# Moving stores from ScalarE's queue to SyncE's in a fused attention and feed-forward kernel

## The chip, the cores and the metric

One NeuronCore of a Trainium2 chip runs the kernel. The metric is device time in microseconds for one execution; a kernel's figure is the median of several runs. Names: PE is TensorE, PEld its loading of weights, DVE is VectorE, ACT is ScalarE, POOL is GpSimd, SP is SyncE. ACT and SP can both issue DMA transfers; their queues are called ACTq and SPq in the trace. "L1283" is a line of that kernel's source, so the numbers differ between kernels.

## The reference

Attention with normalised queries and keys (8 batches, 12 heads, 448 tokens, 64 wide), and a gated feed-forward layer on its output (3584 tokens, 768 to 1536 to 768). The three weight matrices come in as 8-byte floats.

```python
q_n, k_n = rmsnorm(q, g_q), rmsnorm(k, g_k)
attn = softmax(q_n @ k_n.T / 8)                 # 8 x 12 x 448 x 448
x = (attn @ v).transpose(0, 2, 1, 3).reshape(3584, 768)
g = x @ w_gate
out = (g * sigmoid(g) * (x @ w_val)) @ w_out
```

## The kernel before

Each matrix product of the feed-forward layer is made as a 3 x 3 scheme of blocks with 15 products in place of 27. Each product needs a combination of weight blocks, a "side". So the weights are first converted: 24 conversions each load nine 128 x 128 blocks of 8-byte numbers, round them to 4 bytes (two passes on ACT, six on DVE), add and subtract blocks on POOL, and store 15 sides to DRAM. The feed-forward blocks load the sides from there in pieces. Four of the 15 sides are plain weight blocks.

A small planner in the kernel places every piece of work: a piece names its engine, its estimated time, its wished time and what it follows, and the planner fixes the order on each engine at build time. The engines then work strictly in that order.

The program falls into stretches: the early attention (12 pairs of heads, with the first six conversions), then four times an "up" block (480 products, gate and value) and a "down" block (240 products, mixed with the next attention), the last down block alone. The other 18 conversions run in the first up block.

The store of a conversion, in five issues because the plain blocks lie apart from the others; `by_bank` is true for the 18 conversions of the first up block:

```python
queue = nc.scalar if by_bank else nc.sync

def store():
    for i, j, k, m in ((3, 6, 6, 2), (2, 5, 12, 9)):
        queue.dma_start(pair(to, at[k], at[m]), pair(blocks, i, j))
    holes = [*sorted(at[x] for x in (6, 2, 12, 9)), 15]
    for i, j in zip(holes, holes[1:]):
        if j - i > 1:
            queue.dma_start(to[:, i + 1 : j], sides[:, i + 1 : j])

last = add(
    "ACT" if by_bank else "SP", 1.75 if by_bank else 3.0, when, store, after=[last], kb=960
)
```

The store of results, four issues of 56 KB for each transposed tile:

```python
def store():
    for q4 in range(P // C):
        to = out[ds(b * S, S), ds((2 * nn + s) * P + C * q4, C)]
        queue = nc.sync if n == NB - 1 and q4 % 2 else nc.scalar
        queue.dma_start(...)
add("ACT", 1.4 if n < NB - 1 else 0.7, when + 1.4, store, after=[turned], uses=[rows], kb=224)
```

ACT, which issues these, also computes: the exponentials of the attention, the silu of the up blocks, copies out of the matrix banks, and the first two passes of each conversion.

Of the kernel before, what the change touches and what calls it, by code (L numbers as in the profile page):

```python
# [477 lines left out]
def fast(  # L478
# [127 lines left out]
    FRESH = (2, 6, 8, 12, 9)  # L606
    up_sides = [dram.tile([P, 15, 2, NC2, P], F32, name=f"up_sides{g}") for g in range(NG)]
# [89 lines left out]
    def attention(m):  # L697
# [19 lines left out]
        def load(x, src):  # L717
            def emit():
                to = take("qk", (m, x), [P, NC, C])
                for g in range(P // C):  # L720
                    rows = src[b, 2 * c + g // 2][:, ts(g % 2, C)]
                    queue.dma_start(to[ts(g, C)], rows.rearrange("(c i) f -> i c f", i=C))


            both = m < 3 and src is k
            queue = nc.scalar if both else nc.sync
            return add(
                "ACT" if both else "SP", 1.4 if both else 2.4, ready - 28.0, emit, takes=[("qk", (m, x))], kb=224, early=25.0,
                after=[staged.get(PAIRS)],
            )  # L730
# [364 lines left out]
    def convert(key, src, order_of, to, when, place, by_bank):  # L1095
# [6 lines left out]
        dst, raw = places[place][:, 0:VALUES], places[place][:, VALUES:PLACE]  # L1102
# [4 lines left out]
        def load():  # L1107
            to = raw.bitcast(I64).rearrange("p (k n f) -> p k n f", k=3, n=3)
            for k in range(3):
                nc.sync.dma_start(to[:, k], src(k))  # L1110

        loaded = add(
            "SP", 1.8, when - 12.0, load, after=[staged.get(place), *wait], kb=1152, early=3.0
# [41 lines left out]
        alls = raw.rearrange("p (b f) -> p b f", f=P)  # L1155
        sides = alls[:, 0:15]
        b11, b12, b13, b21, b22, b23, b31, b32, b33 = (blocks[:, i] for i in range(9))
        at = {x: i for i, x in enumerate(order_of)}
# [8 lines left out]
        def pair(x, i, j):  # L1167
            return x[:, i : j + 1 : j - i]
# [4 lines left out]

        spare = raw[:, 15 * P : 16 * P]
        for us, op in (
            (0.79, plus(pair(sides, at[10], at[4]), pair(blocks, 1, 7), pair(blocks, 2, 8))),
            (0.79, plus(pair(sides, at[6], at[1]), twice(w[10]), pair(blocks, 0, 3))),
            (0.48, plus(w[14], w[6], b31)),
            (0.48, minus(w[13], b22, w[10])),
            (0.48, minus(w[8], w[4], b23)),  # L1180
            (0.48, plus(w[7], b21, b22)),
            (0.48, minus(w[7], w[8], w[7])),
            (0.79, minus(pair(sides, at[2], at[3]), twice(b13), pair(blocks, 3, 6))),
            (0.48, plus(w[5], w[2], b11)),
            (0.79, minus(pair(alls, at[11], 15), pair(blocks, 7, 8), pair(blocks, 2, 5))),
            (0.48, plus(w[0], spare, b31)),
        ):
            last = add("POOL", us, when, op, after=[last], port=True)


        queue = nc.scalar if by_bank else nc.sync

        def store():
            for i, j, k, m in ((3, 6, 6, 2), (2, 5, 12, 9)):
                queue.dma_start(pair(to, at[k], at[m]), pair(blocks, i, j))
            holes = [*sorted(at[x] for x in (6, 2, 12, 9)), 15]
            for i, j in zip(holes, holes[1:]):
                if j - i > 1:
                    queue.dma_start(to[:, i + 1 : j], sides[:, i + 1 : j])

        last = add(
            "ACT" if by_bank else "SP", 1.75 if by_bank else 3.0, when, store, after=[last], kb=960
# [4 lines left out]
    def up_weights(i, *how):  # L1207

        g, which, c = i // 4, i // 2 % 2, i % 2
        w = (moe_w_gate, moe_w_val)[which].rearrange("(c k p) (n f) -> p c k n f", p=P, k=3, n=3)  # L1210
        weights["up", i] = convert(
            ("up", i), lambda k: w[:, c, k, :, ts(g, P)], UP_ORDER, up_sides[g][:, :, which, c], *how
        )

    def down_weights(i, *how):

        g, s = divmod(i, 2)
        w = moe_w_out.rearrange("(k g p) (n s f) -> p k g n s f", g=NG, p=P, n=3, s=2)
        weights["down", i] = convert(
            ("down", i), lambda k: w[:, k, g, :, s], DOWN_ORDER, down_sides[:, :, s, g], *how  # L1220
        )
# [29 lines left out]

    def block(n):
# [12 lines left out]
        def up_product(g, step, x, which, load, key):  # L1265
# [4 lines left out]
            opens = which and g == 0 and step < 2  # L1270
            bank = (which, b)
# [6 lines left out]
            def emit():  # L1278
                if opens:
                    take(*value_banks[b], [P, TB])  # L1280
                w = tiles[key].rearrange("p (x w c f) -> p x w c f", x=5, w=2, c=NC2)
                for c in range(NC2):
                    nc.tensor.matmul(  # L1283
                        ps(), w[:, step % 5, which, c], xs[:, SLOT[x], c],
                        start=fresh and c == 0, stop=c == NC2 - 1, skip_group_check=True,
                    )
# [87 lines left out]
        def up_load(g, piece):  # L1374
            key = ("ws", (n, g, piece))
            load = add(
                "SP", 0.6, start + (30 * g + 10 * piece) * unit - 24.0,
                lambda: nc.sync.dma_start(
                    take(*key, [P, 10 * NC2 * P]),
                    up_sides[g][:, ts(piece, 5)].rearrange("p x w c f -> p (x w c f)"),  # L1380
                ),
                after=[*last_load, *(weights["up", 4 * g + i] for i in range(4))], takes=[key], kb=1280,
                early=8.0,
            )
            last_load[:] = [load]
            return key, load
# [52 lines left out]
        def down_product(step, x, s):  # L1439
# [5 lines left out]
            if piece not in loads:  # L1445
                loads[piece] = add(
                    "SP", 0.6, when - 24.0,
                    lambda: nc.sync.dma_start(
                        take(*key, [P, 10 * NC2 * P])[:, 0 : size * 2 * NG * P],
                        down_sides[:, ds(2 * piece, size)].rearrange("p x s g f -> p (x s g f)"),  # L1450
                    ),
# [6 lines left out]
            def emit():  # L1458
                w = tiles[key][:, 0 : size * 2 * NG * P]
                w = w.rearrange("p (x s g f) -> p x s g f", s=2, g=NG, f=P)  # L1460
                for g in range(NG):
                    nc.tensor.matmul(  # L1462
                        banks[s][:, 0:S], w[:, step % 2, s, g], where[x][:, g],
                        start=fresh and g == 0, stop=g == NG - 1, skip_group_check=True,
                    )
# [50 lines left out]
            def store():  # L1516
                for q4 in range(P // C):
                    to = out[ds(b * S, S), ds((2 * nn + s) * P + C * q4, C)]
                    queue = nc.sync if n == NB - 1 and q4 % 2 else nc.scalar
# [6 lines left out]
                "ACT", 1.4 if n < NB - 1 else 0.7, when + 1.4, store, after=[turned], uses=[rows],  # L1526
# [30 lines left out]
    for t, x in ((gq2, g_q), (gk2, g_k)):  # L1557
        col = x.rearrange("(d one) -> d one", one=1)
        nc.scalar.dma_start(t[0:64, :], col)
        nc.scalar.dma_start(t[64:128, :], col)  # L1560
# [95 lines left out]
```

## Time and profile before

| | us |
|---|---|
| median of 4 runs, in the rounds with the changed kernel | 1533.06 (1528.9 to 1538.2) |
| span of the profiled execution | 1529.4 |
| TensorE busy in it | 1439.6 (94%) |

The first view is the busy time by stretch, cut where TensorE's work changes kind: the stretch and its length, then busy us (and instructions) of PE, PEld, DVE, ACT and POOL, the mean granted clock of TensorE (1.00 is full speed), the DMA share (the mean busy share of the 16 DMA engines) and GB/s. Shown are the early attention, the first up block, the second down block and the third up block.

```profile
0.00:152.00 152.00, 110.42 (x1201) 49.39 (x1202) 99.59 (x175) 92.35 (x181) 57.50 (x92) 0.97 0.68 164
152.00:367.50 215.50, 190.66 (x490) 92.09 (x489) 158.16 (x239) 87.87 (x127) 115.02 (x207) 0.95 0.82 253
...
730.40:890.30 159.90, 156.57 (x988) 70.65 (x984) 112.10 (x161) 98.15 (x223) 62.90 (x38) 0.99 0.43 96
890.30:1088.00 197.70, 194.19 (x601) 95.97 (x601) 92.30 (x159) 70.88 (x135) 11.52 (x10) 0.98 0.35 101
```

The length less PE's busy time is idle time: 41.6, 24.8, 3.3 and 3.5 us here. A clock below 1.00 means that part of PE's busy time is slow work.

The second view is the timeline: start, duration, engine, line, operation, and in brackets how long the engine had been idle and what ended it.

```profile
878.55 8.54 ACTq L1520 DMA_DIRECT2D out_dram<-spare  x8
880.22 9.84 SPq L1378 DMA_DIRECT2D ws<-up_sides  x2
...
887.14 0.53 ACT L989 COPY xs<-at 128x448 f32<-128x448 f32 x1 [8.87 <-DMA out_dram<-spare]
...
894.83 1.86 PE L1283 MATMUL mm<-xs,ws 128*128 128x448 f32 x2 [3.48 <-DVE xs L1030]
```

Eight issues of results keep ACT's queue for 8.54 us. The issues themselves take 4.1 us of this. The longest wait between two of them, 3.2 us, ends at 886.77, which is 0.02 us after the first of SP's two loads of sides (1.28 MB, issued at 880.22) has landed; the second load is issued only at 889.74. So ACT's issue seems to wait for a transfer of another queue; why is not shown. The copy of an attention result, next in ACT's order, waits 8.87 us for them, and through VectorE's division and combinations TensorE waits 3.48 us.

### The profile page before, as it was taken

The page shows a single profiled execution, that of the slowest core. Times are in us where ns is not written, and L with a number is a line of the kernel's source. Part 1 is how long each engine was busy: PE and PEld are TensorE (multiplying, and loading weights), DVE is VectorE, ACT ScalarE, POOL GpSimd, SP SyncE. Part 2 cuts the span into 40 slices and gives each one's busy share as a digit, 9 for nine tenths or more (in the row PEclk, how much of TensorE's full clock was granted, in tenths as well). Part 3 has the DMA queues.
Part 4 walks back from the last instruction along what each step waited for, and adds up shares of the span by engine and source line. Part 5 has one row for each costly group of instructions (what it writes and reads, how often), then busy time and mean ns, then how long its engine had stood idle before and what let it go on. Part 6 is the DMA issues. An engine that isn't in the chain of part 4 may idle for free.

```text
span 1529.4 us, 19374 instructions
## 1 busy us (share of the span) xinstructions
PE 1439.6 (94%) x6672; PEld 683.1 (45%) x6672; DVE 912.1 (60%) x1405; ACT 679.7 (44%) x1366; POOL 397.0 (26%) x440
## 2 busy tenths in 40 slices
PE   3888989879999999999999989999999989999998
PEld 1334444434444445554444445554444435555554
DVE  3868877667886743455886643444786744323533
ACT  5765434335876422255776422135767532222100
POOL 1553755553543300002444300002344310000000
PEclk9999999989999999999999999999999999999999
DMA  7567888974454342343454342343344342222235
GB/s 152 132 152 223 274 290 270 292 206 133 105 105 106 65 143 75 112 113 88 101 120 98 60 127 69 109 113 109 79 111 109 78 110 89 85 101 72 83 95 104
DMA packets 408240, 193.28 MB, mean 126 GB/s; under 512 B 324164, under 2 KB 397892, under 8 KB 398404
## 3 DMA queue, kind: packets, MB, share of 16 engines
q1 hardware_dynamic: 288288, 163.92, 38.6%
q10 hardware_dynamic: 119844, 28.04, 8.5%
q8 instruction: 54, 0.88, 0.3%
q14 instruction: 54, 0.44, 0.1%
HBM read 157.29 MB, written 34.60 MB: 125 GB/s over the span
## 4 chain that ended last, share of the span: by engine, by line
PE 65%; DVE 5%; ACT 2%; issue 2%; DMA 1%; ACTq 1%; SPq 1%; POOL 0%; DVEq 0%; POOLq 0%
PE mm L1283 18%; PE at L1283 18%; PE mm L1462 18%; PE st L834 5%; PE at L910 4%; ACTq L1520 1%; PE st L934 1%; ACT spare L984 1%; ACT es L849 1%; DMA out_dram<-spare 1%; DVE spare L1510 1%; DVE sums L860 1%; DVE rd L969 1%; DMA ws<-down_sides 0%; DVE xs L996 0%
## 5 line engine op out<-in xcount | busy, mean ns | idle before, releaser
L1283 PE MATMUL mm<-xs,ws 128*128 128x448 f32 x960 | 409.4, 549 | 30.4 <-DVE gt L1250 17.2
L1283 PE MATMUL at<-xs,ws 128*128 128x448 f32 x960 | 404.7, 544 | 2.7 <-DVE v L1248 1.6
L1283 PEld LDWEIGHTS mm<-xs,ws 128*128 128x128 f32 x960 | 182.8, 192 | 218.4 <-issue 167.2
L1283 PEld LDWEIGHTS at<-xs,ws 128*128 128x128 f32 x960 | 183.9, 192 | 186.5 <-issue 177.3
L789 POOL TENSOR_TENSOR work<-work,rr 128x448 f32<-128x448 f32 x96 | 99.1, 1053 | 539.2 <-DVE rr L680 377.6
L834 PE MATMUL st<-work 64*64 64x448 f32 (+1 forms) x1536 | 154.6, 508 | 29.3 <-ACT work L808 20.4
L1462 PE MATMUL mm<-gt,ws 128*128 128x448 f32 x448 | 177.4, 548 | 0.0
L1246 DVE TENSOR_TENSOR gt<-gt,mm 128x448 f32<-128x448 f32 x64 | 39.7, 620 | 207.2 <-PE mm L1283 200.2
L1462 PE MATMUL mm<-hs,ws 128*128 128x448 f32 x384 | 151.0, 544 | 0.0
L849 ACT ACTIVATE es<-st 128x896 f32<-128x896 f32 x129 | 114.4, 914 | 80.0 <-PE at L910 31.0
L1357 ACT ACTIVATE st<-gt 128x448 f32<-128x448 f32 x96 | 52.5, 547 | 205.1 <-DVE gt L1250 96.2
L984 ACT COPY spare<-rd 32x224 f32<-32x224 f32 x288 | 108.1, 375 | 40.0 <-DVE rd L969 34.9
L854 POOL TENSOR_TENSOR sums<-es 128x896 f32<-128x896 f32 x36 | 75.2, 2089 | 180.4 <-PE st L934 82.0
L1462 PEld LDWEIGHTS mm<-gt,ws 128*128 128x128 f32 x448 | 84.2, 191 | 84.4 <-issue 82.6
L910 PE MATMUL at<-es,v 64*64 64x448 f32 x1032 | 112.6, 543 | 4.5 <-ACT es L849 2.6
L1244 ACT COPY gt<-mm 128x448 f32<-128x448 f32 x80 | 42.5, 531 | 156.8 <-PE mm L1283 153.0
L1462 PEld LDWEIGHTS mm<-hs,ws 128*128 128x128 f32 x384 | 71.3, 190 | 71.8 <-issue 70.1
L834 PEld LDWEIGHTS st<-work 64*64 64x64 f32 x1536 | 51.7, 134 | 104.8 <-issue 36.3
L1244 ACT COPY v<-at 128x448 f32<-128x448 f32 x96 | 51.0, 532 | 82.1 <-PE at L1283 65.3
L805 DVE STREAM_TRANSPOSE work<-work 128x448 f32<-128x448 f32 x96 | 59.7, 632 | 29.8 <-POOL work L789 21.1
L854 POOL TENSOR_TENSOR sums<-sums,es 128x896 f32<-128x896 f32 x36 | 75.7, 2103 | 2.8
L1360 DVE SCALAR_TENSOR_TENSOR gt<-st,v 128x448 f32<-128x448 f32 x96 | 59.7, 622 | 16.9 <-ACT st L1357 10.0
(137 smaller groups left out, 1541.9 us busy)
## 6 DMA issues: line engine op xcount, KB each, us to landing
ws<-up_sides SPq DMA_DIRECT2D x48, 1280.0 KB, 5.7
ws<-down_sides SPq DMA_DIRECT2D x28, 1024.0 KB, 5.0
work<-in_q_dram SPq DMA_DIRECT2D x192, 56.0 KB, 2.5
work<-in_k_dram SPq DMA_DIRECT2D x180, 56.0 KB, 2.4
out_dram<-spare ACTq DMA_DIRECT2D x168, 56.0 KB, 2.0
v<-in_v_dram SPq DMA_DIRECT2D x96, 96.0 KB, 2.5
es<-in_moe_w_out_dram SPq DMA_DIRECT2D x9, 384.0 KB, 6.6
v<-in_v_dram SPq DMA_DIRECT2D x96, 32.0 KB, 2.3
```

The source lines that it names most:

```text
L789: nc.gpsimd.tensor_tensor(out=tiles["t", m][:, x], in0=tiles["qk", (m, x)], in1=rr.to_broadcast([P, NC, C]), op=ALU.mult,)
L805: nc.vector.transpose(to, tiles["t", m][:, x].rearrange("p c f -> p (c f)"))
L834: nc.tensor.matmul(st[ds(D * x, D), h, 0:n], tiles["KT", m][rows, ds(P * j + D * of_keys, D)], tiles["QT", m][rows, ds(Q * of_queries, n)] ...
L849: nc.scalar.activation(e, tiles["st", (m, j)][:, :, 0 : S * width(j) // P], AF.Exp)
L854: nc.gpsimd.tensor_tensor(out=to, in0=tiles["e", (m, 0)] if j == 1 else to, in1=e, op=ALU.add)
L910: nc.tensor.matmul(tiles["at", (m, x)][ds(D * h, D), queries], tiles["v", m][rows, j, h], tiles["e", (m, j)][rows, h], start=j == 0, stop= ...
L984: nc.scalar.copy(inv[ds(D * h + C * to, C), ts(x, Q)], tiles["rd", m][ds(D * h + C * x, C)])
L1244: nc.scalar.copy(to, ps)
L1283: nc.tensor.matmul(ps(), w[:, step % 5, which, c], xs[:, SLOT[x], c], start=fresh and c == 0, stop=c == NC2 - 1, skip_group_check=True,)
L1357: nc.scalar.activation(take(*act, [P, 2, TB])[:, 0, 0:S], to, AF.Silu)
L1360: nc.vector.scalar_tensor_tensor(to, tiles[act][:, 0, 0:S], 1.0 / SCALE, tiles[ready], op0=ALU.mult, op1=ALU.mult,)
L1462: nc.tensor.matmul(banks[s][:, 0:S], w[:, step % 2, s, g], where[x][:, g], start=fresh and g == 0, stop=g == NG - 1, skip_group_check=True,)
```

## The change

The intent: all stores of sides and nearly all of results go to SP; the sides are built so that the 11 computed ones and the four plain ones are neighbours in SBUF and in DRAM, so that one issue stores all 15; the loads of sides, which now find some of their sides apart, are split in two where needed; and the first loads are spread over SP, ACT and GpSimd.

```diff
-            both = m < 3 and src is k            # pairs whose k is loaded by ACT
+            both = m == 0 and src is k
...
+    UP_SUMS = (8, 1, 7, 10, 13, 14, 3, 5, 11, 0, 4)
+    DOWN_SUMS = (1, 10, 14, 3, 11, 0, 4, 5, 8, 7, 13)
+    BLOCKS = (6, 2, 12, 9)                        # the plain blocks, last
...
-            for k in range(3):
-                nc.sync.dma_start(to[:, k], src(k))
+            for i, n, rows in ((0, 2, (1, 3, 0)), (2, 2, (0, 2, 2)), (5, 3, (0, 3, 1))):
+                nc.sync.dma_start(to[:, i : i + n], src(slice(*rows[:2]), rows[2]))
+            for i, k, n in ((4, 0, 0), (8, 2, 2)):
+                nc.sync.dma_start(to[:, i], src(k, n))
...
-            "ACT" if by_bank else "SP", 1.75 if by_bank else 3.0, when, store, after=[last], kb=960
+            "SP", 0.6, when, lambda: nc.sync.dma_start(to, sides), after=[last], kb=960,
...                                               # loads of sides: one or two issues a piece
+        for names, first in ((sums, 0), (BLOCKS, len(sums))):
+            here = sorted(names.index(x) for x in part if x in names)
+            if here:
+                src = sides[:, ds(first + here[0], len(here))]
+                nc.sync.dma_start(...)
...
-                    queue = nc.sync if n == NB - 1 and q4 % 2 else nc.scalar
+                    queue = nc.scalar if n == NB - 1 and q4 % 2 else nc.sync
...
-                "ACT", 1.4 if n < NB - 1 else 0.7, when + 1.4, store, after=[turned], ...
+                "SP", 2.4 if n < NB - 1 else 1.2, when + 1.4, store, after=[turned], ...
...
-        nc.scalar.dma_start(t[0:64, :], col)      # gains, 4 such loads
+        nc.gpsimd.dma_start(t[0:64, :], col)
```

Since the planner is told of other engines and times, the order on every engine changes a little too.

More of the change, by code (lines that the diff above doesn't have):

```diff
@@ L606, in fast @@
     FRESH = (2, 6, 8, 12, 9)
+    UP_SUMS = (8, 1, 7, 10, 13, 14, 3, 5, 11, 0, 4)
+    DOWN_SUMS = (1, 10, 14, 3, 11, 0, 4, 5, 8, 7, 13)
+    BLOCKS = (6, 2, 12, 9)
+    WS = 10 * NC2 * P
     up_sides = [dram.tile([P, 15, 2, NC2, P], F32, name=f"up_sides{g}") for g in range(NG)]
@@ L1093, in fast, with convert @@
     GT, HS, ES, XS, PAIRS, SPARE = (0, 1, 2), 3, 4, (5, 6), 7, 8
-    def convert(key, src, order_of, to, when, place, by_bank):
+    def convert(key, src, sums, to, when, place, by_bank):
         rank = 20.0 if by_bank else 0.0
@@ L1100, in add @@
             return order.add(*what, **dict(rank=rank, **more))
-        dst, raw = places[place][:, 0:VALUES], places[place][:, VALUES:PLACE]
+        raw, dst = places[place][:, 0 : 2 * VALUES], places[place][:, 2 * VALUES : PLACE]
         words = raw.bitcast(U32).rearrange("p (n two) -> p n two", two=2)
@@ L1107, in load @@
         def load():
-            to = raw.bitcast(I64).rearrange("p (k n f) -> p k n f", k=3, n=3)
-            for k in range(3):
-                nc.sync.dma_start(to[:, k], src(k))
+            to = raw.bitcast(I64).rearrange("p (b f) -> p b f", f=P)
+            for i, n, rows in ((0, 2, (1, 3, 0)), (2, 2, (0, 2, 2)), (5, 3, (0, 3, 1))):
+                nc.sync.dma_start(to[:, i : i + n], src(slice(*rows[:2]), rows[2]))
+            for i, k, n in ((4, 0, 0), (8, 2, 2)):
+                nc.sync.dma_start(to[:, i], src(k, n))
         loaded = add(
-            "SP", 1.8, when - 12.0, load, after=[staged.get(place), *wait], kb=1152, early=3.0
+            "SP", 2.5, when - 12.0, load, after=[staged.get(place), *wait], kb=1152, early=3.0
         )
@@ L1154, in convert @@
         blocks = dst.rearrange("p (b f) -> p b f", f=P)
-        alls = raw.rearrange("p (b f) -> p b f", f=P)
-        sides = alls[:, 0:15]
-        b11, b12, b13, b21, b22, b23, b31, b32, b33 = (blocks[:, i] for i in range(9))
-        at = {x: i for i, x in enumerate(order_of)}
+        b21, b31, b13, b23, b11, b12, b22, b32, b33 = (blocks[:, i] for i in range(9))
+        sides = places[place].rearrange("p (b f) -> p b f", f=P)[:, 7:22]
+        at = {x: i for i, x in enumerate(sums)}
         w = {x: sides[:, i] for x, i in at.items()}
@@ L1171, in twice @@
             return x.rearrange("p (one f) -> p one f", one=1).to_broadcast([P, 2, P])
-        spare = raw[:, 15 * P : 16 * P]
         for us, op in (
-            (0.79, plus(pair(sides, at[10], at[4]), pair(blocks, 1, 7), pair(blocks, 2, 8))),
-            (0.79, plus(pair(sides, at[6], at[1]), twice(w[10]), pair(blocks, 0, 3))),
-            (0.48, plus(w[14], w[6], b31)),
+            (0.79, plus(pair(sides, at[10], at[4]), pair(blocks, 5, 7), pair(blocks, 2, 8))),
+            (0.79, plus(pair(sides, at[1], at[14]), twice(w[10]), pair(blocks, 0, 4))),
+            (0.48, plus(w[14], w[14], b31)),
             (0.48, minus(w[13], b22, w[10])),
@@ L1182, in convert @@
             (0.48, minus(w[7], w[8], w[7])),
-            (0.79, minus(pair(sides, at[2], at[3]), twice(b13), pair(blocks, 3, 6))),
-            (0.48, plus(w[5], w[2], b11)),
-            (0.79, minus(pair(alls, at[11], 15), pair(blocks, 7, 8), pair(blocks, 2, 5))),
-            (0.48, plus(w[0], spare, b31)),
+            (0.48, minus(w[3], b13, b31)),
+            (0.48, minus(w[5], b13, b21)),
+            (0.48, plus(w[5], w[5], b11)),
+            (0.79, minus(pair(sides, at[11], at[0]), pair(blocks, 7, 8), pair(blocks, 2, 3))),
+            (0.48, plus(w[0], w[0], b31)),
         ):
             last = add("POOL", us, when, op, after=[last], port=True)
-        queue = nc.scalar if by_bank else nc.sync
-        def store():
-            for i, j, k, m in ((3, 6, 6, 2), (2, 5, 12, 9)):
-                queue.dma_start(pair(to, at[k], at[m]), pair(blocks, i, j))
-            holes = [*sorted(at[x] for x in (6, 2, 12, 9)), 15]
-            for i, j in zip(holes, holes[1:]):
-                if j - i > 1:
-                    queue.dma_start(to[:, i + 1 : j], sides[:, i + 1 : j])
         last = add(
-            "ACT" if by_bank else "SP", 1.75 if by_bank else 3.0, when, store, after=[last], kb=960
+            "SP", 0.6, when, lambda: nc.sync.dma_start(to, sides), after=[last], kb=960,
         )
@@ L1211, in up_weights @@
         weights["up", i] = convert(
-            ("up", i), lambda k: w[:, c, k, :, ts(g, P)], UP_ORDER, up_sides[g][:, :, which, c], *how
+            ("up", i), lambda k, n: w[:, c, k, n, ts(g, P)], UP_SUMS, up_sides[g][:, :, which, c],
+            *how,
         )
@@ L1219, in down_weights @@
         weights["down", i] = convert(
-            ("down", i), lambda k: w[:, k, g, :, s], DOWN_ORDER, down_sides[:, :, s, g], *how
+            ("down", i), lambda k, n: w[:, k, g, n, s], DOWN_SUMS, down_sides[:, :, s, g], *how
         )
@@ L1250, in read, with load_sides, place_of @@
             nc.vector.tensor_tensor(out=to, in0=ps, in1=old, op=ALU.subtract)
+    def load_sides(key, sides, part, sums):
+        size = 2 * (NC2 if sums is UP_SUMS else NG) * P
+        to = take(*key, [P, WS])[:, 0 : len(part) * size].rearrange("p (x f) -> p x f", f=size)
+        i = 0
+        for names, first in ((sums, 0), (BLOCKS, len(sums))):
+            here = sorted(names.index(x) for x in part if x in names)
+            if here:
+                size = len(here)
+                src = sides[:, ds(first + here[0], size)]
+                nc.sync.dma_start(to[:, ds(i, size)], src.rearrange("p x a b f -> p x (a b f)"))
+                i += size
+    def place_of(x, part, sums):
+        mine = [*(y for y in sums if y in part), *(y for y in BLOCKS if y in part)]
+        return mine.index(x)
     def block(n):
@@ L1270, in up_product @@
             opens = which and g == 0 and step < 2
+            at = place_of(x, UP_ORDER[step - step % 5 :][:5], UP_SUMS)
             bank = (which, b)
@@ L1280, in emit @@
                     take(*value_banks[b], [P, TB])
-                w = tiles[key].rearrange("p (x w c f) -> p x w c f", x=5, w=2, c=NC2)
+                w = tiles[key].rearrange("p (x w c f) -> p x w c f", w=2, c=NC2, f=P)
                 for c in range(NC2):
                     nc.tensor.matmul(
-                        ps(), w[:, step % 5, which, c], xs[:, SLOT[x], c],
+                        ps(), w[:, at, which, c], xs[:, SLOT[x], c],
                         start=fresh and c == 0, stop=c == NC2 - 1, skip_group_check=True,
@@ L1376, in up_load @@
             load = add(
-                "SP", 0.6, start + (30 * g + 10 * piece) * unit - 24.0,
-                lambda: nc.sync.dma_start(
-                    take(*key, [P, 10 * NC2 * P]),
-                    up_sides[g][:, ts(piece, 5)].rearrange("p x w c f -> p (x w c f)"),
-                ),
+                "SP", 1.2, start + (30 * g + 10 * piece) * unit - 24.0,
+                lambda: load_sides(key, up_sides[g], UP_ORDER[5 * piece :][:5], UP_SUMS),
                 after=[*last_load, *(weights["up", 4 * g + i] for i in range(4))], takes=[key], kb=1280,
@@ L1446, in down_product @@
                 loads[piece] = add(
-                    "SP", 0.6, when - 24.0,
-                    lambda: nc.sync.dma_start(
-                        take(*key, [P, 10 * NC2 * P])[:, 0 : size * 2 * NG * P],
-                        down_sides[:, ds(2 * piece, size)].rearrange("p x s g f -> p (x s g f)"),
-                    ),
+                    "SP", 0.9, when - 24.0,
+                    lambda: load_sides(key, down_sides, DOWN_ORDER[2 * piece :][:2], DOWN_SUMS),
                     after=[*last_load, *(weights["down", i] for i in range(2 * NG))], takes=[key],
@@ L1458, in emit @@
             def emit():
-                w = tiles[key][:, 0 : size * 2 * NG * P]
+                w = tiles[key][:, 0 : 4 * NG * P]
                 w = w.rearrange("p (x s g f) -> p x s g f", s=2, g=NG, f=P)
+                at = place_of(x, DOWN_ORDER[step - step % 2 :][:2], DOWN_SUMS)
                 for g in range(NG):
                     nc.tensor.matmul(
-                        banks[s][:, 0:S], w[:, step % 2, s, g], where[x][:, g],
+                        banks[s][:, 0:S], w[:, at, s, g], where[x][:, g],
                         start=fresh and g == 0, stop=g == NG - 1, skip_group_check=True,
@@ L1525, in down_product @@
             add(
-                "ACT", 1.4 if n < NB - 1 else 0.7, when + 1.4, store, after=[turned], uses=[rows],
+                "SP", 2.4 if n < NB - 1 else 1.2, when + 1.4, store, after=[turned], uses=[rows],
                 kb=224,
@@ L1558, in fast @@
         col = x.rearrange("(d one) -> d one", one=1)
-        nc.scalar.dma_start(t[0:64, :], col)
-        nc.scalar.dma_start(t[64:128, :], col)
+        nc.gpsimd.dma_start(t[0:64, :], col)
+        nc.gpsimd.dma_start(t[64:128, :], col)
     nc.vector.memset(chosen, 0.0)
```

## The prediction

> **What bounds the kernel now.** I read the page's busy shares first: TensorE is busy for 1439.6 of 1529.4 us, so whatever this change gains has to come out of the 90 us in which TensorE stands idle, plus the time in which it runs slowly after an idle spell. Next I cut the span at the places where TensorE goes from one kind of work to another (busy time by stretch: PE, PEld, DVE, ACT, POOL with counts, then the granted clock, the DMA share and GB/s):
>
> ```profile
> 0.00:153.00 153.00, 111.42 (x1202) 49.57 (x1202) 100.40 (x177) 92.77 (x182) 58.42 (x95) 0.96 0.69 164
> 153.00:357.00 204.00, 179.16 (x454) 86.86 (x454) 148.51 (x223) 83.74 (x121) 114.10 (x205) 0.95 0.86 264
> 357.00:539.00 182.00, 178.30 (x1131) 77.25 (x1130) 142.00 (x206) 118.73 (x267) 75.65 (x46) 1.00 0.45 98
> 539.00:722.00 183.00, 183.00 (x523) 91.43 (x523) 81.95 (x144) 63.37 (x121) 11.53 (x10) 1.00 0.36 103
> ```
>
> The first stretch is the early attention, the second the first up block, in which 18 of the 24 weight conversions are still running. The later up blocks (the fourth line is one) have no idle TensorE at all. So the idle time is 42 us in the first stretch, 25 us in the second, and some 23 us in everything after: 4 in the third, 7 and 5 in the two later down stretches, 7 at the very end. The first up block really ends at 367.5; its 480 products at 1.504 us per four need 180.5 us and take 214.
>
> Then the timeline at the two longest gaps of that block, to see who held TensorE:
>
> ```profile
> 187.93 4.23 ACTq L1199 DMA_DIRECT2D up_sides<-gt  x3
> 192.21 0.55 ACT L1357 ACTIVATE st<-gt 128x448 f32<-128x448 f32 x1 [6.87 <-DMA up_sides<-gt]
> 192.78 0.62 DVE L1360 SCALAR_TENSOR_TENSOR gt<-st,v 128x448 f32<-128x448 f32 x1 [4.92 <-ACT st L1357]
> ...
> 203.41 1.86 PE L1283 MATMUL mm<-xs,ws 128*128 128x448 f32 x2 [6.14 <-DVE gt L1250]
> ```
>
> ```profile
> 301.83 5.20 ACTq L1199 DMA_DIRECT2D down_sides<-spare  x3
> ...
> 307.07 0.55 ACT L1357 ACTIVATE st<-gt 128x448 f32<-128x448 f32 x1 [7.40 <-DMA down_sides<-spare]
> 307.65 0.62 DVE L1360 SCALAR_TENSOR_TENSOR gt<-st,v 128x448 f32<-128x448 f32 x1 [2.64 <-ACT st L1357]
> ...
> 315.35 3.35 PE L1283 MATMUL mm<-xs,ws 128*128 128x448 f32 x4 [9.60 <-DVE gt L1250]
> ```
>
> Read these downwards. Three store issues keep ACT's queue for 4 to 5 us; the silu behind them is late; DVE, which works in program order, idles for it, and then has the late reads and two rounding passes (4.7 us for a tile) to do in a row; TensorE waits for its bank to be read. The list of waits blames "DVE gt L1250" (17.2 us), but the first cause is ACT holding stores. After each long gap the first four products take 3.35 us instead of 1.67.
>
> Last, the start and one block change:
>
> ```profile
> 4.13 5.42 ACTq L722 DMA_DIRECT2D work<-in_k_dram  x8
> 17.62 2.52 PE L834 MATMUL st<-work 64*64 64x224 f32 x16 [17.62 <-ACT work L808]
> 22.03 0.23 ACT L672 ACTIVATE rr<-ss 128x28 f32<-128x28 f32 x1 [4.46 <-DMA work<-in_k_dram]
> 23.00 3.19 PE L834 MATMUL st<-work 64*64 64x448 f32 x16 [2.85 <-ACT more L849]
> ```
>
> ```profile
> 865.28 5.35 ACTq L1520 DMA_DIRECT2D out_dram<-spare  x7
> ...
> 870.73 0.92 ACT L849 ACTIVATE es<-st 128x896 f32<-128x896 f32 x1 [5.36 <-DMA out_dram<-spare]
> ...
> 871.70 0.59 PE L934 MATMUL st<-sums,many 128*32 128x224 f32 x8 [2.03 <-ACT es L849]
> ```
>
> **What the Trainium skill says.** "DMA: Bandwidth & Descriptors", section "Issuing engines are not separate DMA queues": issues from several engines run on the same 16 DMA engines, and spreading them only saves issue time on the sequencer, "usually small relative to the DMA itself". The first half agrees with the DMA share of 0.86 in the first up block; the second doesn't hold here: 89 store issues held ACT's queue for 20.2 + 52.5 = 72.7 us in that block, 0.8 us each, up to 5.4 us for three. "ScalarE: Activation LUTs", section "What ACT_TABLE_LOAD costs", gives 1283 ns for a table load; the trace has 1.28 us. "TensorE: Matmul & The Clock Gate", Part 1, says that the array falls to half clock after an idle window of about 3.4 us; the products after the 6.14 and 9.60 us gaps ran at half pace, which agrees.
>
> **The change, part by part.** The build order of both kernels shows what moves. TensorE's instructions are the same in number and nearly in order, so 1439.6 us of work stays.
> - *Weights' stores.* Five issues for each conversion become one of 960 KB, and all go to SP. ACT loses 90 issues, 72.7 us of queue time. What counts is the part that reached TensorE: 6.14 + 9.60 us idle, and 1.7 + 1.7 + 0.5 us of slow products behind them, 19.6 us. The gaps under 2 us in this block (some 8 us) come mainly from DVE's program order and I leave them. I count two thirds of 19.6, **-13 us**, because the second gap has the rounding of another tile in DVE's order, which stays, and because of DMA: in 153 to 357 it moves 264 GB/s at a share of 0.86. Each conversion takes 1.15 + 0.96 MB and its share of the loads back; the same bytes in 13 us less ask for about 0.92. That can be done (single 10 us stretches reach 1.0 and over 330 GB/s), but there is little left.
> - *More issues on SP.* Conversion loads 3 to 5 (48 more in all), loads of sides 80 to 140, 144 stores of results, 8 k loads; the six conversions that SP already stored go from 30 issues to 6, and 18 new ones come. At 0.35 to 0.6 us each, as the same kinds of issue take on SP now, the 250 more are about 120 us over a span in which SP mostly waits for free buffers: 0 on the path by itself.
> - *GpSimd.* The combination of sides has 12 operations in place of 11, three pairs in place of four: about +0.2 us for each of 24, POOL being busy 26%: 0.
> - *First loads.* Four gain loads leave ACT (4 x 0.6 us), so the first k arrives 2.4 us sooner; and the third pair's k no longer blocks ACT for 5.01 us, which cost the 2.85 us gap. 5.3 us, of which the SP queue, now with 8 more issues, gives some back: **-4 us**.
> - *Results' stores.* 144 issues leave ACT (0.5 to 0.76 us each, about 100 us). On the path lay 2.03 and 0.56 us before the totals near 871 and 1228, and gaps under 0.7 us before exponentials: **-4 us**. The 3.5 us at 895 and 1249 stay: there DVE's transposition waits until a result store has landed (4.79 and 5.02 us), and on SP that store will sit behind a 1.28 MB load of sides.
> - *Table loads.* The order on ACT has 28 of them in place of 22, all six extra at the first block's end, where silu and exp now alternate: 7.7 us of ACT, of which I put **+2 us** on the path.
>
> Sum: -13 - 4 - 4 + 2 = -19, from 1531.7 to about **1512 us**, 1.2% faster.
>
> **The rivals.**
> 1. *SP becomes the wait.* Stores wait on SP for GpSimd or DVE, and everything behind them, above all the loads of sides, waits too. For it: SP is in order, and in the first up block it gets 18 stores that each may hold it for 4 us. Against it: a piece of sides is asked for 15 us before use and lands in 5.7 us. If it bites, the 13 us shrink to zero or new gaps of "DMA ws" appear: 1525 to 1540.
> 2. *Everything that ACT held comes back.* Then also the small gaps and the slow clock of the first block go, and the early stretch gains: 25 + 4 in the block, 5 + 4 elsewhere: 1494 to 1500, just over 2%.
> 3. *It is hidden anyway.* After 368 us TensorE has almost no idle time, so 100 us taken from ACT there yield nothing, and in the first block DMA takes over as the bound at a share near 1: 1520 to 1526.
>
> **Range and chances.** I hold my own sum for likeliest, then rival 3, then 2, then 1. The first up block may gain 0 to 25 us, the rest may gain 12 or lose 4; taken together I leave a tenth below 1496 (nearly all of rival 2) and a tenth above 1530 (rival 1). Faster by over 2% means below 1501: 0.18. Slower by over 2% needs a new wait of 30 us more than is gained: 0.03.
>
> **What would show it.** Right: no ACT wait on DMA of sides or results; the gaps of 6 and 9.6 us before L1283 gone or under 3; DMA share of the first up block near 0.92; first product near 15 us; up blocks two to four unchanged at 182 to 183 us. Wrong: TensorE waiting for the loads of sides, SP waiting for GpSimd while buffers are free, or a long gap near 350 with table loads ahead of it. The number fails if the early attention shortens by more than 10 us, or if the gaps just move to another product.

## The result, and the profile after

The changed kernel took 1495.87 us (1494.33 to 1499.07, 4 runs) against 1533.06 us in the same rounds. The ratio is 0.9759, with a 95% interval of 0.9724 to 0.9794: 2.4% faster. A ratio here is taken over the fast runs of both kernels in the same rounds, so it is not quite the ratio of the medians.

The forecast of 1512 us was 16 us too high, and the measured time lies just under 1496 us, below which the prediction had left a tenth. "Within 2%" had been given 0.79, and the result was faster by over 2%, which had 0.18.

The same stretches of the changed kernel, busy time by stretch, columns as before:

```profile
0.00:149.30 149.30, 115.21 (x1201) 49.27 (x1202) 99.57 (x175) 92.23 (x181) 64.89 (x105) 0.92 0.68 161
149.30:353.80 204.50, 188.74 (x506) 92.26 (x505) 159.58 (x244) 97.58 (x138) 118.60 (x224) 0.97 0.89 272
...
717.80:871.90 154.10, 154.10 (x988) 70.49 (x985) 113.43 (x163) 101.12 (x229) 63.41 (x38) 1.00 0.45 100
871.90:1064.10 192.20, 191.70 (x602) 94.82 (x600) 91.40 (x158) 68.46 (x128) 11.53 (x10) 1.00 0.37 104
```

The first up block is 11.0 us shorter. The second down block and the third up block have lost nearly all idle time and all of the slow clock: 5.8 and 5.5 us. The early attention lost 7.5 us of idle time (41.6 to 34.1) but worked at a clock of 0.92 where it had 0.97, so its busy time grew by 4.8 us and it gained only 2.7 us. (The profiled execution is the slowest of the four, 1499.07 us; the others took 1494.33 to 1496.45.)

The timeline at the change from the second down block to the third up block, of the changed kernel:

```profile
862.95 0.92 SPq L1260 DMA_DIRECT2D ws<-up_sides  x2
...
864.08 8.30 SPq L1531 DMA_DIRECT2D out_dram<-spare  x8
...
865.41 0.53 ACT L995 COPY xs<-at 128x448 f32<-128x448 f32 x1 [3.60 <-PE at L916]
...
873.35 1.02 PE L1299 MATMUL mm<-xs,ws 128*128 128x448 f32 x2 [0.50 <-DVE xs L1036]
```

Eight issues of results still need 8.30 us, again with a wait between two of them (3.5 us), but SP spends them. ACT makes its copy as soon as TensorE has delivered, and TensorE's gap is 0.50 us in place of 3.48.

The two long gaps of the first up block, of the changed kernel:

```profile
192.03 0.53 SPq L1199 DMA_DIRECT2D up_sides<-hs  x1
...
195.93 2.61 PE L1299 MATMUL mm<-xs,ws 128*128 128x448 f32 x3 [3.17 <-DVE gt L1248]
```

```profile
292.60 0.75 DVE L1147 TENSOR_SCALAR st<-work 128x576 uint32<-128x576 uint32 x1
...
296.71 0.75 DVE L1153 CUSTOM_DVE_ANT_0 work<-work,st 128x1152 uint16<-128x1152 uint16 x1
297.38 0.62 DVE L1248 TENSOR_TENSOR gt<-mm,gt 128x448 f32<-128x448 f32 x1
...
298.05 2.61 PE L1299 MATMUL mm<-xs,ws 128*128 128x448 f32 x3 [6.72 <-DVE gt L1248]
```

They have shrunk from 6.14 and 9.60 us to 3.17 and 6.72. What is left of the second is VectorE rounding a tile (six operations, 292.60 to 297.4) ahead of the read for which TensorE waits. (In both views the window ends after three products.) A store of 960 KB now is one issue of 0.53 us.

At the start, the changed kernel's first k load and first product:

```profile
1.63 2.00 ACTq L728 DMA_DIRECT2D work<-in_k_dram  x4
14.66 4.54 PE L840 MATMUL st<-work 64*64 64x224 f32 x32 [14.66 <-ACT work L814]
```

The k load is issued 2.5 us sooner (1.63 against 4.13) and the first product comes 2.96 us sooner (14.66 against 17.62).

The lengths of all stretches, read off the traces in the same way (start of a block's first product to that of the next); all in us, from the one profiled execution of each:

| kernel | early | up 1 | down 1 | up 2 | down 2 | up 3 | down 3 | up 4 |
|---|---|---|---|---|---|---|---|---|
| before | 152.0 | 215.5 | 171.5 | 191.4 | 159.9 | 197.7 | 157.0 | 186.8 |
| changed | 149.3 | 204.5 | 172.6 | 191.4 | 154.1 | 192.2 | 154.1 | 181.2 |
| e1, same order, stores on SP | 153.5 | 200.6 | 168.9 | 191.5 | 154.1 | 192.1 | 154.1 | 181.2 |
| e2, results on SP | 152.4 | 214.8 | 169.0 | 191.5 | 154.1 | 192.2 | 154.1 | 181.2 |
| e3, sides alone | 158.5 | 199.6 | 175.4 | 191.5 | 156.8 | 196.9 | 155.8 | 186.0 |
| e4, first loads alone | 144.0 | 219.6 | 170.7 | 191.4 | 159.8 | 197.9 | 157.0 | 187.0 |
| e5, sides on SP, five issues | 156.6 | 201.9 | 172.7 | 191.4 | 158.0 | 196.9 | 156.7 | 187.0 |
| e6, sides on ACT, one issue | 156.9 | 198.1 | 175.0 | 191.5 | 156.9 | 198.2 | 155.9 | 185.9 |
| e7, e1 and first loads | 141.6 | 211.1 | 168.1 | 191.4 | 154.3 | 192.1 | 154.2 | 181.1 |
| e8, changed without the layout | 142.1 | 216.3 | 166.1 | 191.5 | 154.1 | 192.1 | 154.2 | 181.1 |
| e9, more DMA | 148.3 | 207.3 | 172.9 | 191.4 | 154.2 | 192.1 | 154.1 | 181.2 |
| e10, less VectorE | 147.6 | 194.0 | 173.4 | 191.4 | 154.1 | 192.2 | 154.1 | 181.2 |
| e11, three parts | 146.6 | 216.3 | 166.6 | 191.4 | 154.2 | 192.1 | 154.2 | 181.1 |
| e12, e7 with less VectorE | 141.4 | 198.8 | 168.8 | 191.5 | 154.2 | 192.2 | 154.1 | 181.2 |

From down 2 to up 4 the changed kernel gains 5.8 + 5.5 + 2.9 + 5.6 = 19.8 us. That is where the forecast fell short.

### The profile page after: what moved, and what is told of

Read it like the earlier page. It is cut to its first block, busy times and chain, and to the rows that moved or that the text cites.

```text
span 1497.2 us, 19504 instructions
## 1 busy us (share of the span) xinstructions
PE 1434.6 (96%) x6672; PEld 681.5 (46%) x6672; DVE 916.9 (61%) x1405; ACT 689.8 (46%) x1372; POOL 408.8 (27%) x468
## 4 chain that ended last, share of the span: by engine, by line
PE 73%; DVE 3%; ACT 1%; issue 1%; DMA 0%; SPq 0%; DVEq 0%; ACTq 0%
PE mm L1473 22%; PE mm L1299 19%; PE at L1299 19%; PE st L840 6%; PE at L916 6%; PE st L940 1%; DVE ss L684 0%; DMA out_dram<-spare 0%; ACT es L855 0%; DVE sums L866 0%; DVE ss L768 0%; DVE rd L975 0%; DVE ss L782 0%; DVE hs L1040 0%; ACT spare L990 0%
## 5 line engine op out<-in xcount | busy, mean ns | idle before, releaser
L1299 PE MATMUL mm<-xs,ws 128*128 128x448 f32 x960 | 405.0, 544 | 15.9 <-DVE gt L1248 9.9
L916 PEld LDWEIGHTS at<-es,v 64*64 64x64 f32 x1032 | 40.9, 138 | 67.7 <-issue 59.2
```

Of the source, the lines that this page charges most:

```text
L916: nc.tensor.matmul(tiles["at", (m, x)][ds(D * h, D), queries], tiles["v", m][rows, j, h], tiles["e", (m, j)][rows, h], start=j == 0, stop= ...
L1299: nc.tensor.matmul(ps(), w[:, at, which, c], xs[:, SLOT[x], c], start=fresh and c == 0, stop=c == NC2 - 1, skip_group_check=True,)
```

## The experiments

Theory A: the cause of the gain is that ACT's in-order queue is no longer held by issuing stores, so that the computations behind the stores start in time. Rivals: B, the planner's new order makes the gain; C, the number of issues counts, not the queue. Later, for what remains in the first up block: D, DMA binds it, and E, VectorE's rounding does. All runs had five rounds; all kernels gave correct results.

### e1: only the queue, nothing else

```diff
 # the kernel before; the add("ACT", ...) lines are untouched, so the planner orders as before
-        queue = nc.scalar if by_bank else nc.sync
+        queue = nc.sync
...
-                    queue = nc.sync if n == NB - 1 and q4 % 2 else nc.scalar
+                    queue = nc.scalar if n == NB - 1 and q4 % 2 == 0 else nc.sync
```

Expected:

> The kernel before with one thing changed: the 90 stores of sides and the 144 stores of results that ACT issued are issued by SP, at the same place of the program; five issues for a conversion stay, first loads stay, and the order of the instructions on TensorE, VectorE, GpSimd and (but for the stores) ACT is exactly that of before. Theory A (ACT's queue was held by store issues, and all behind it waited): most of the gain comes, 22 to 34 us faster than before, the 3.5 us gaps at the block changes gone. Theory B (the gain comes from the new order that the kernel's own planner made): less than 10 us faster. Theory C (one issue in place of five is what counts, as SP would otherwise be held): SP's 5 issues delay the loads of sides, 0 to 10 us faster or slower, with TensorE waiting for loads of sides.

Measured: 1497.72 us against 1532.35, ratio 0.9773 (0.9759 to 0.9787). The timeline of e1 at the first up block's gaps (from two windows) and the block change:

```profile
199.72 1.77 PE L1283 MATMUL mm<-xs,ws 128*128 128x448 f32 x4 [3.03 <-DVE gt L1250]
302.49 3.35 PE L1283 MATMUL mm<-xs,ws 128*128 128x448 f32 x4 [7.06 <-DVE gt L1250]
```

```profile
860.72 8.30 SPq L1520 DMA_DIRECT2D out_dram<-spare  x8
...
870.00 1.02 PE L1283 MATMUL mm<-xs,ws 128*128 128x448 f32 x2 [0.50 <-DVE xs L1030]
```

The gaps look like the changed kernel's, with the order of PE, DVE and POOL exactly that of the kernel before, and ACT's too but for the stores taken out. The gain of some 34.6 us is just above what A expected (22 to 34). 2.27% of the 2.41% come from the queue alone; the two intervals overlap. Rival B falls. The new layout, the split loads and the first loads add nothing that these runs can tell.

### e2: only the results' stores

```diff
-                    queue = nc.sync if n == NB - 1 and q4 % 2 else nc.scalar
+                    queue = nc.scalar if n == NB - 1 and q4 % 2 else nc.sync
-                "ACT", 1.4 if n < NB - 1 else 0.7, when + 1.4, store, ...
+                "SP", 2.4 if n < NB - 1 else 1.2, when + 1.4, store, ...
```

Expected:

> The kernel before with only the results' stores on SP, planned there. The prediction gave this part 4 us. The trace of the changed kernel suggests about 20 us: the later down and up stretches are 5.8, 5.5, 2.9 and 5.6 us shorter, and in the kernel before ACT was held for 8.5 us by eight stores at a block's end. Theory A: 15 to 22 us faster than before, first up block unchanged at about 215 us. If the prediction's reading (the wait is for the landing of a store, which stays) were right: 2 to 6 us.

Measured: 1515.30 us against 1532.35, ratio 0.9882 (0.9866 to 0.9898), 1.2% or 18 us. The first up block stays at 214.8 us, and the later stretches are those of the changed kernel to a tenth of a microsecond. The part to which the forecast gave 4 us is worth 18, half of the whole.

### e3: only the sides

The changed kernel with results and first loads put back (the last three hunks of the diff and its first undone).

Expected:

> The kernel before with only the sides' part: new layout, one store each on SP, two loads for most pieces; results and first loads as before. Theory A: 9 to 15 us faster, all of it in the first up block (215 to about 204 us), the later stretches as before with their 3.5 us gaps. Rival (parts are not additive, as the later gaps come from the loads of sides in the same rings): also the later stretches get shorter.

Measured: 1523.31 us against 1532.35, ratio 0.9948 (0.9934 to 0.9963), 8 us, just under the expected 9 to 15. The first up block gains 15.9 us, more than expected, but the early attention loses 6.5 us and the first down block 3.9. In the early attention TensorE idles 46.9 us (158.5 less 111.6 busy) against 41.6. The later gaps of 3.49 us stay, at 886 and 1239 us, but the stretches from down 2 to up 4 still lose 5.9 us together, so the parts are not wholly apart, as the rival had it.

### e4: only the first loads

```diff
-            both = m < 3 and src is k
+            both = m == 0 and src is k
...
-        nc.scalar.dma_start(t[0:64, :], col)
-        nc.scalar.dma_start(t[64:128, :], col)
+        nc.gpsimd.dma_start(t[0:64, :], col)
+        nc.gpsimd.dma_start(t[64:128, :], col)
```

Expected:

> The kernel before with only the first loads changed: gains by GpSimd's queue, the second and third pair's k by SP. Theory A: first product at about 14.7 us in place of 17.6, 2 to 5 us faster in all. Rival (the early stretch is bound by something else than its start, as the start came 3 us sooner and the stretch ended 2.7 us sooner with more idle in between): 0 to 2 us.

Measured: 1524.85 us against 1532.35, ratio 0.9952 (0.9939 to 0.9965), 7 us, above both expectations. The first product comes at 14.67 us and the early attention ends 8.0 us sooner; the first up block gives 4.1 us of it back.

The three parts add to 1.18 + 0.52 + 0.48 = 2.2%, against 2.4% for all.

### e5 and e6: five issues on SP, or one on ACT

e5 is the kernel before with the conversions' stores planned on SP; e6 is e3 with the single store issued by ACT in the first up block:

```diff
 # e5
-        queue = nc.scalar if by_bank else nc.sync
+        queue = nc.sync
-            "ACT" if by_bank else "SP", 1.75 if by_bank else 3.0, when, store, ...
+            "SP", 3.0, when, store, ...
 # e6
-            "SP", 0.6, when, lambda: nc.sync.dma_start(to, sides), ...
+            "ACT" if by_bank else "SP", 0.35 if by_bank else 0.6, when,
+            lambda: (nc.scalar if by_bank else nc.sync).dma_start(to, sides), ...
```

Expected:

> The kernel before with the conversions' stores planned on SP, but in the old layout: five issues each, three loads each, no split loads of sides. Theory A (it is enough that ACT is not held): 12 to 18 us faster than before, early stretch unchanged near 152 us, first up block near 200 us. Theory C (the one issue matters): the 72 us of issue time now hold SP, the first up block stays over 208 us, under 8 us faster.

> The sides' part in the new layout with one issue each, but ACT issues the 18 stores of the first up block. In the changed kernel 19 such stores held SP for 11.2 us in all, 0.6 us each; before, 89 held ACT for 72.7 us. Theory C (fewer issues are as good as another queue): as e3_sides_only, 6 to 12 us faster than before, first up block near 200 us, ACT held for about 11 us. Theory A in its strict form (the stores have to leave ACT): at most 3 us faster, as ACT is still blocked for several us per store.

Measured: e5 1520.08 us, ratio 0.9910 (0.9896 to 0.9923); e6 1525.01 us, ratio 0.9947 (0.9934 to 0.9961); before 1532.95. Both cures work: the first up block falls to 201.9 and 198.1 us. In e6's trace 18 stores hold ACT for 9.6 us where 89 had held it for 72.7 us, and it is as fast as e3, whose stores SP issues. In e5 some 95 issues hold SP for about 90 us, and the first up block doesn't suffer; the early attention is 4.6 us longer than before, as it is in e3 and e6 (6.5 and 4.9), and why is not shown. So for the sides neither "off ACT" nor "one issue" is needed on its own: what counts is ACT's queue time. The strict form of theory A (the stores have to leave ACT) falls, and so does C. Of the three, e5, which keeps the old layout, is the fastest, and its interval lies below those of e3 and e6: by itself the new layout costs some 0.4% here.

### e7 and e8: the rest without the layout

e7 is e1 with e4's edit. e8 is the changed kernel without the layout: e5 with e2's and e4's edits.

Expected:

> The kernel of e1 (all stores on SP in the old layout and at the old places of the program) with the changed first loads, so without the new layout. Parts add: 1532 - 34.6 - 7.5 = about 1490, some 5 us below the changed kernel. If the early gain of the first loads is eaten as in the changed kernel (whose early stretch was 149.3 where e4 had 144.0): 1495 to 1498.

> The changed kernel with its new layout undone: all stores on SP as the planner places them, first loads as changed, but five issues and three loads for a conversion, and whole loads of sides. It measures what the layout is worth in the end. Theory A says nothing or a small loss: 1488 to 1496, as the layout's early cost (e3's early stretch was 158.5 against 152) goes too. Theory C: slower than the changed kernel by over 5 us, as SP is held by five issues per conversion.

Measured: e7 1494.79 us, ratio 0.9756 (0.9743 to 0.9769); e8 1497.69 us, ratio 0.9767 (0.9745 to 0.9788). The head start of the first loads is there (early attention 141.6 and 142.1 us), and the first up block eats it (211.1 and 216.3). e8 lies a little above what A expected. Against the changed kernel's 0.9759 the layout is worth nothing that can be told. In e7 one of the new gaps waits for a load of sides:

```profile
193.56 3.35 PE L1283 MATMUL mm<-xs,ws 128*128 128x448 f32 x4 [4.53 <-DMA ws<-up_sides]
```

In the kernels with all stores off ACT the first down block starts at 352.7 (e7), 353.8 (changed), 354.1 (e1) and 358.4 us (e8), although the early attention ends between 141.6 and 153.5. Something other than the start sets that time.

### e9 and e10: what binds the first up block now

e9 stores four of the 15 blocks of each of the 18 conversions a second time, to an unused place. e10 leaves out the last rounding operation (the result is then truncated, not rounded, in 18 of the 24 conversions; it is a probe).

```diff
 # e9, in the changed kernel
+    extras = dram.tile([24, P, 4, P], F32, name="extras")
...
+        def store():
+            nc.sync.dma_start(to, sides)
+            if by_bank:
+                nc.sync.dma_start(extras[next(extra_at)], sides[:, 0:4])
 # e10, in the changed kernel, for by_bank
-            nc.vector.scalar_tensor_tensor(to, hi[:, part], 0x80000000, to, ...)
-            nc.vector.tensor_tensor(out=bits[:, part], in0=to, in1=lo[:, part], op=ALU.add)
+            nc.vector.scalar_tensor_tensor(bits[:, part], hi[:, part], 0x80000000, to, ...)
```

Expected:

> The changed kernel, with the same order on all engines, that stores 4 of the 15 blocks of each of the 18 conversions of the first up block a second time, into an unused place: 18 x 256 KB = 4.7 MB, at the 306 GB/s of that stretch 15 us of DMA. In all kernels with the stores off ACT the first down block starts at 353 to 358 us, however early the block before it starts. Theory D (DMA is the bound there now): 8 to 15 us slower than the changed kernel, down block at 362 to 369. Theory E (the rounding on VectorE in its program order is the bound): 0 to 4 us slower.

> The changed kernel, planned in the same order, without the third VectorE operation of the rounding in the 18 conversions of the first up block (it truncates instead of rounding: results off in the last bits). That takes 36 x 0.75 = 27 us of work from VectorE there. Theory E (VectorE's rounding between the reads is the bound of the first up block): the 6.7 us gap near 298 shrinks to under 5, 8 to 15 us faster than the changed kernel. Theory D: 0 to 4 us faster.

Measured: e9 1497.28 us, ratio 0.9772 (0.9752 to 0.9793); e10 1488.13 us, ratio 0.9705 (0.9691 to 0.9720). The first 100 us of the first up block, busy time by stretch, columns as before, for the changed kernel, e9 and e10 in turn:

```profile
150.00:250.00 100.00, 95.89 (x251) 47.89 (x250) 85.32 (x129) 48.25 (x63) 63.21 (x123) 0.98 0.96 306
```

```profile
150.00:250.00 100.00, 96.74 (x249) 48.45 (x250) 84.10 (x127) 47.92 (x63) 62.17 (x121) 0.97 1.01 324
```

```profile
150.00:250.00 100.00, 98.76 (x264) 49.72 (x263) 71.55 (x110) 50.69 (x67) 68.07 (x133) 1.00 1.01 325
```

In e9 DMA moves 324 GB/s in place of 306 and TensorE is no less busy; its first up block takes 207.3 us against 204.5, and the whole costs 1 to 2 us, within the scatter, where D had asked for 8 to 15. DMA at a share of 0.96 was not the bound, and D falls. In e10 VectorE does less, TensorE is busy for 98.8 of 100 us, and the block is 10.5 us shorter (194.0 against 204.5); its longest gap falls from 6.72 to 4.17 us. E holds, at 8 us for the whole kernel, at the low end of what was expected.

### e11 and e12: attempts at a faster kernel

e11 cuts the rounding of a conversion in three parts in place of two. e12 is e7 with e10's edit.

```diff
 # e11, in the changed kernel
-                part = ts(k, VALUES // 2)
+                part = ts(k, VALUES // 3)
...
-        for k in range(2):
-            last = add("DVE", 2.28 if by_bank else 1.85, ...)
+        for k in range(3 if by_bank else 2):
+            last = add("DVE", 1.75 if by_bank else 1.85, ...)
```

Expected:

> An attempt at a faster kernel: the changed kernel with the rounding of a conversion in three parts in place of two, so that VectorE can read a bank between them. It adds 18 x 3 instructions, some 8 us of VectorE, and four table loads more in the planner's order. Theory E: the 6.7 us gap falls under 4 us and the kernel is 0 to 8 us faster than the changed one; theory D: same or some us slower.

> The kernel of e7 (old layout, stores on SP at the old places, first loads changed; early stretch 141.6 us, first up block 211 us) with the VectorE operation taken away as in e10. If VectorE is what ate the head start of the first loads in e7, the first up block falls to 195 to 203 us, and the whole to 1479 to 1487 us, faster than e10 (1488). If what binds that block in e7 is the loads of sides behind five issues (it had a 4.5 us wait for one): 1487 to 1492.

Measured: e11 1502.14 us, ratio 0.9796 (0.9783 to 0.9810), slower than the changed kernel's 0.9759 (the intervals overlap a little, but each of its five runs is slower than all four of the changed kernel): the gaps became 6.26 and 7.26 us, and the first up block 216.3. Smaller parts did not let the reads in between: in the trace all three parts, nine operations from 296.30 to 301.68, still stand ahead of the read that ends the second gap. e12 took 1484.07 us against 1532.98, ratio 0.9684 (0.9661 to 0.9707), 3.2% faster than before and the lowest of all, though its interval overlaps that of e10; its first up block is 198.8 us, as expected if VectorE had eaten the head start in e7. It truncates most of the weights where the others round; whoever needs the last bit should take e7 or the changed kernel, which can't be told apart.

## Why the prediction was right or wrong

- **What bounds the kernel: right.** TensorE's work stayed (1434.6 us busy against 1439.6), and the gain is idle time and slow clock. The reading of the first up block, stores that hold ACT, silu late, VectorE idle and then in a bunch, is shown by e1 (queue alone) and e6 (fewer issues on ACT).
- **Weights' stores, -13 us, and table loads, +2 us: the mechanism right, the sum hit by luck.** The block fell by 11.0 us, but not where the sum had it. Of the two gaps, 15.7 us, only 5.9 went where two thirds were to go: 3.17 and 6.72 us stayed, over the "gone or under 3" that the prediction named as its own sign. Another 3.2 us came from the small gaps, which it had left as they were, and 1.9 us from busy time. The sides alone took 15.9 us from the block (e3), and the first loads gave 4.1 us back (e4), which was not in this sum. That VectorE's rounding keeps the rest was right, as e10 confirms. The reason given beside it, that DMA has little left, was wrong: e9 moved 6% more per second at no cost that can be told.
- **Results' stores, -4 us: wrong, and the step that failed.** The prediction kept the gaps: "The 3.5 us at 895 and 1249 stay: there DVE's transposition waits until a result store has landed". Measured alone the part is worth 18 us (e2). The chain of waits had named the landing of the store, but the line of the timeline shown above shows ACT itself held by eight issues for 8.54 us, and its copy late by 8.87. Freed of them, ACT delivers and the gap is 0.50 us; the transposition at that place (890.30 before, 869.79 after) has no idle time before it in either trace. The slow clock was left out as well: up 3 and up 4 lost 5.5 and 5.6 us each, where the gap itself was 3.5.
- **First loads, -4 us: 2.7 us of the early stretch in the full change,** where the clock granted in the profiled execution was 0.92; alone they gave 7 us (e4). Why the clock is lower in that trace is not settled; e10, with the same loads, had 0.95.
- **Table loads.** All 28 stand where the build order put them. The first down block takes 172.6 to 173.4 us in the kernels with 28 and results on SP (changed, e9, e10), and 166.1 to 169.0 in those with 22 (e1, e2, e7, e8, e12). That would fit a cost of some 4 us, not 2, but e11 has 32 table loads and takes 166.6 us there. In the changed kernel, e9 and e10 two of the loads fall into the first down block, in e11 and the kernels with 22 none. No run changed the table loads alone, so their cost stays open.
- **SP with 250 more issues, 0 us: right.** Rival 1 (SP becomes the wait) did not come about in the changed kernel; e7 shows one wait of its kind, 4.53 us.
- **Rival 2** (all that ACT held comes back, "5 + 4 elsewhere", 1494 to 1500 us) hit the number by another sum, less in the first up block and 20 us elsewhere, so its hit is luck. **Rival 3** (after 368 us nothing is to be gained) falls with e2, which gained 18 us, nearly all of it after 368 us.
- **The signs named beforehand.** No wait of ACT for stores in its list of waits and a first product near 15 us (14.66) came true; gaps under 3 us and unchanged later up blocks (5.5 and 5.6 us shorter) did not, and the DMA share of the first up block was 0.89 where 0.92 had been asked.

## What to carry to other kernels

In these traces ACT, which computes and issues DMA, does both in one order, so issues that stall delay the computation behind them (8.87 us at the block change). Look in the timeline at how long the issues hold the queue where the queue is full, not at their usual cost, and ask of each late computation whether the engine itself stood in an issue: a list of waits names only the last releaser. Give the stores to an engine that computes nothing, or make them few; after that, look for the next in-order engine, here VectorE.

## What the Trainium skill lacked or had wrong

- "DMA: Bandwidth & Descriptors", section "Issuing engines are not separate DMA queues", says that issuing from several engines "will only save the time on the sequencer", usually small. Here the time on the sequencer, with the waits between its issues, was nearly the whole effect: moving 234 issues from one sequencer to another, in an unchanged order, made the kernel 2.3% faster (e1).
- The same page lacks that an issue can stand in its queue, it seems until an earlier transfer, of another queue too, has landed. Four issues of results took 1.94 us in free stretches (0.5 us each); eight took 8.54 us with one load of 1.28 MB in flight, and three stores of sides took 5.20 us (at 301.83), of which 1.4 us are the issues and 3.7 us one wait that ends at 306.66, 0.02 us after a weight load of SP's landed. Of the nine waits of over 0.8 us between two stores of ACT from 170 to 890 us, five end 0.02 us after a landing, four times that of a transfer from SP.
- It also lacks that the hold goes by issues more than by bytes: a store of 960 KB held a queue for 0.53 us as one issue (18 of them 9.6 us in e6), while five issues for the same bytes took about 4 us (89 for 72.7 us, some 52 us of it the issues themselves).
- "TensorE: Matmul & The Clock Gate", Part 1, gives an idle window of about 3.4 us before the clock halves. By the trace, whose ends of products are modelled, a gap of 3.17 us was enough in the changed kernel (the four products after it took 3.28 us in place of 1.67); a gap of 3.03 us was not in e1 (1.77 us), and one of 3.04 us was in e4 (3.33 us, at 298.41).
